# Rounding double-precision weights with the sign in the exponent: a clamp and a sloped rectifier in place of magnitude, minimum and sign steps, under newly ordered lists

## The chip, the core and the metric

The kernel runs on one core of a Trainium2 chip. A core has a matrix engine (TensorE, PE in the profile), a vector engine (VectorE, DVE), a scalar engine with function tables (ScalarE, ACT), GpSimd (POOL) and SyncE (SP), which here only issues transfers. Each engine works through its own list of instructions in order and waits on semaphores. The metric is device microseconds (us) of one execution. Three runs of the kernel before took 552.08, 551.65 and 548.6 us: the median is 551.65.

## The reference

Two layers stand behind one another. The first is a gated linear recurrence with complex gates, per batch (4) and head (8), over 768 steps with states of 48x48; the second is a maxout layer on its output.

```python
for t in range(S):                       # S = 768, D = 48
    ar, ai = (a_re_n[:, :, t, :, None], a_im_n[:, :, t, :, None])
    new_re = ar * S_re - ai * S_im
    new_im = ar * S_im + ai * S_re
    S_re, S_im = (new_re + kv, new_im)   # kv: outer product of k[t], v[t]
    y[:, :, t] = np.einsum('bhd,bhde->bhe', q[:, :, t], S_re)
# second layer: x is y as (3072, 384)
h = np.maximum(np.maximum(x @ w1, x @ w2), x @ w3)   # w1..w3: (384, 768)
return (h @ w_out).astype(np.float32)                # w_out: (768, 384)
```

The gates are first limited to a magnitude of 0.999. The four weight matrices come in double precision (64 bits each); q, k, v and the gates are single precision.

## The kernel before, in words

**Groups and chunks.** Time is cut into 12 groups (g = 0 to 11) of 64 steps. A group has two chunks, x and y, of two batch rows each. For each group the gates' logarithms and phases are worked out ("gates" and "angles": Square, Ln, Exp, Relu, Arctan and Sin on ScalarE, products on VectorE), summed along time by matmuls (`sums`, `cs`, `F`), and turned into factors. Then k and q are scaled, transposed (`tp`), scored against one another (`A`, `B`), masked into `atm`, and multiplied with v and the carried state (`y`, `dk`, with states in `g`).

**The second layer.** It is computed as x·w1·w_out plus max(0, x(w2-w1), x(w3-w1))·w_out. So w1 is kept negated, added to w2 and w3 (step g below), and the product w1·w_out (`wp`) is formed once (`T`, `t`, `M`, `m` words: transposes `wt`, products `wm`). `U..` words are the up matmuls into `up`, `u..` words take the maximum; from group 1 on the output matmuls run as seven products of half size (`P1` to `P7`, sums `S1` to `S4` in the tile called strassen, additions `r..`, `ox`, `oy`, `oz`).

**Weights.** There are 12 blocks (0 to 11) of 128 partitions x 768 weights: 0, 3, 6 of w1, 1, 4, 7 of w2, 2, 5, 8 of w3, 9 to 11 of w_out. `weight_load` (word `WL`) brings a raw block of 768 KB into a room that several blocks share (`ROOMS`): H and S, the upper parts of w2, w3 and w_out. Each weight lies there as two 32-bit words, low and high. `weight_step` (line 419 on) then rounds it to single precision, one word of the list for each step:

- a: ScalarE writes the magnitude of the high word, read as a float and scaled by 2^-112, into `ex` (a part of the tile xhx that two blocks take turns in, `EX`).
- b: VectorE takes the minimum with LAST.
- c: VectorE shifts left by three bits, which makes the 64-bit exponent a 32-bit one; for w1 it also sets the sign bit.
- e: VectorE puts the top three bits of the low word underneath.
- f: VectorE brings in the sign of the high word and writes the weight to its place.
- g: for w2 and w3 only, the block of w1 is added, on VectorE or by an adding transfer of POOL.

**Order.** No scheduler decides the order. `SCHEDULE` (line 21 on) is a list of words such as `Wb3:0` (step b of block 3) or `Ax:2` (scores of chunk x of group 2); `program` runs it from left to right, and each engine gets its instructions in that order (the class `Bound` ties each to the one before). `SLOTS` gives each PSUM tile one of four slots. `OTHER` is a set of words that run on their second engine: magnitudes and copies on VectorE instead of ScalarE, loads of q, k, v on POOL's queue instead of SP's, additions on VectorE instead of an adding transfer of POOL. `activation` loads a new table on ScalarE when the next function is in the other one of two sets (Exp and Ln in one, Sin and Arctan in the other); Abs, Relu, Square and Copy run in either.

Nearly all instructions carry line 198, that of the recording helper, so groups are told apart by their tiles.

Of the kernel before, what the change touches and what calls it, by code (L numbers as in the profile page):

```python
# [26 lines left out]
xor:1 Enx:0 Eqx:0 lnL:1 Wc9:0 Ekx:0 tx:0 relu:1 mkx:0 csy:0 expe:1 We9:0 nfx:0 expw:1 sumsy:0 Lix:2 ty:0 Wf9:0 abs:1
T2:0 nfy:0 mqx:0 half:1 afx:0 Wa10:0 Wa11:0 Lvy:0 t2:0 Wb10:0 Wb11:0 Wc10:0 Wc11:0 We10:0 sax:0 We11:0 pw:1 sbx:0
uqx:0 tpqx:0 lnw:1 t0:0 Wf11:0 WL1:0 T1:0 WL2:0 Wf10:0 expL:1 Qcx:0 Lky:0 ukx:0 tpkx:0 mulw:1 Wa1:0 t1:0 Cdx:0 Lvx:0
Eqy:0 Kcx:0 Wa2:0 lne:1 Q2x:0 Fy:0 f2y:0 Wb1:0 f1y:0 WL4:0 kEnx:0 Q1x:0 M0:0 f3y:0 Liy:2 f0y:0 Eny:0 mulai:1 Wb2:0  # L30
afy:0 Ax:0 Wc1:0 stt:1 We1:0 mqy:0 Wc2:0 Wf1:0 We2:0 Eky:0 say:0 QBx:0 sqi:2 KBx:0 Lnop:1 sby:0 Wa4:0 Wf2:0 g0x:0
dkx:0 Lrx:2 Lry:2 sqr:2 add:2 atan:1 lnL:2 Wb4:0 Cdy:0 turn:1 WL5:0 Wg1:0 Wc4:0 M1:0 h1x:0 expe:2 cs:1 relu:2 g1x:0
Liy:3 expw:2 t:1 Wa5:0 abs:2 lne:2 We4:0 g2x:0 mky:0 Wf4:0 uky:0 M2:0 g3x:0 Bx:0 Wb5:0 nfx:1 Wc5:0 m1:0 Z3:0 b1x:0
tpky:0 Zh:0 uqy:0 nfy:1 b0x:0 tpqy:0 We5:0 Wg4:0 Lix:3 F:1 Kcy:0 yx:0 Lqy:1 Qcy:0 Wf5:0 xor:2 m0:0 Q2y:0 xx:0 addw:2
Q1y:0 KBy:0 WL7:0 f1:1 f0:1 QBy:0 Wg2:0 sumsx:1 Enx:1 WL8:0 half:2 Cdx:1 Ekx:1 Cdy:1 U11x:0 u11x:0 Lqx:1 lnw:2 Ay:0
Wa7:0 g0y:0 Eqx:1 expL:2 af:1 U01x:0 Wb7:0 f2:1 u01x:0 U02x:0 g1y:0 By:0 mulai:2 Wg5:0 g2y:0 Wc7:0 Wa8:0 g3y:0 We7:0
b0y:0 Lky:1 b1y:0 kEny:0 Wf7:0 sumsy:1 f3:1 yy:0 mulw:2 xy:0 sb:1 dky:0 u02x:0 stt:2 U02y:0 Lkx:1 h1y:0 Z4:0 mqx:1
atan:2 U11y:0 Lnop:2 Wb8:0 mkx:1 turn:2 sa:1 ukx:1 u11y:0 U01y:0 U12y:0 u01y:0 Eky:1 uqx:1 u02y:0 Eqy:1 cs:2 u12y:0
tpqx:1 Wc8:0 We8:0 mky:1 Eny:1 Lky:2 tpkx:1 Qcx:1 Wf8:0 t:2 Wg7:0 U21y:0 Wg8:0 U21x:0 nfy:2 nfx:2 Q1x:1 Lqx:2 mqy:1
Q2x:1 kEnx:1 uqy:1 u21y:0 U22y:0 u22y:0 u21x:0 af:2 Kcx:1 sumsx:2 F:2 Ax:1 g0x:1 g1x:1 g2x:1 Ekx:2 Enx:2 Eqx:2 Z2:0  # L40
Lvx:1 f1:2 f3:2 KBx:1 h0x:1 uky:1 tpqy:1 f2:2 Qcy:1 Q1y:1 g3x:1 Oy:0 Lvy:2 tpky:1 Q2y:1 mqx:2 Lvy:1 f0:2 Lkx:2 sa:2
sqi:3 oy:0 Lry:3 J3:0 QBx:1 dkx:1 Bx:1 sb:2 h1x:1 U12x:0 QBy:1 uqx:2 QGx:1 U22x:0 Kcy:1 KBy:1 Lrx:3 Lqy:2 u22x:0
u12x:0 Ay:1 b1x:1 g0y:1 g1y:1 g2y:1 g3y:1 b0x:1 mkx:2 sqr:3 tpqx:2 Qcx:2 By:1 yx:1 add:3 lnL:3 QBx:2 expe:3 b0y:1
sumsy:2 xx:1 Eqy:2 Eky:2 expw:3 relu:3 Q1x:2 b1y:1 QGy:1 abs:3 Ox:0 Q2x:2 Lix:4 ukx:2 ox:0 mky:2 mqy:2 Dy:0 uky:2 yy:1
addw:3 tpky:2 lne:3 kEny:1 tpkx:2 Liy:4 Lnop:3 xy:1 xor:3 half:3 Cdy:2 Kcy:2 U11:1 Cdx:2 J1:0 U01:1 Lqx:3 Lrx:4 uqy:2
lnw:3 Kcx:2 KBx:2 J2:0 expL:3 u11:1 Dx:0 Eny:2 mulw:3 mulai:3 stt:3 kEny:2 h0y:1 tpqy:2 atan:3 Lry:4 sqi:4 turn:3
Qcy:2 dky:1 h1y:1 kEnx:2 sumsx:3 u01:1 J4:0 cs:3 Eqx:3 mqx:3 Ax:2 h0y:2 Ekx:3 t:3 sqr:4 add:4 g0x:2 g1x:2 g2x:2 U12:1
Enx:3 Lrx:5 nfx:3 U02:1 lnL:4 expe:4 Q1y:2 nfy:3 expw:4 u12:1 S3:1 af:3 dky:2 g3x:2 relu:4 abs:4 addw:4 Q2y:2 F:3
u02:1 Bx:2 Ay:2 Lvx:2 sb:3 S1:1 f2:3 Lkx:3 h1y:2 f1:3 QGx:2 Lqy:3 P5:1 S2:1 P7:1 f0:3 QBy:2 g0y:2 KBy:2 g1y:2 f3:3
S4:1 lnw:4 g2y:2 P1:1 expL:4 h0x:2 P6:1 r1:1 b0x:2 b1x:2 g3y:2 r6:1 dkx:2 r5:1 r7:1 lne:4 Lry:5 sa:3 Lky:3 r57:1 h1x:2  # L50
sumsy:3 By:2 xor:4 mkx:3 b1y:2 b0y:2 Eny:3 half:4 Cdy:3 Liy:5 yx:2 xx:2 mulw:4 Eky:3 Eqy:3 Py:1 QGy:2 Px:1 P4:1 P3:1
# [5 lines left out]
Qcx:4 dky:3 kEnx:3 dkx:3 S1:2 h1y:3 sumsy:4 S2:2 P5:2 h1x:3 Eqy:4 QBy:3 Dx:1 abs:5 Liy:6 addw:5 b0x:3 b1x:3 lne:5
Lnop:5 half:5 Eky:4 mky:4 Eny:4 mqy:4 Cdx:4 S4:2 Cdy:4 P1:2 P6:2 Py:2 P4:2 r1:2 yx:3 r6:2 r5:2 By:3 lnw:5 expL:5 b0y:3
mulw:5 uqy:4 h0x:4 b1y:3 mulai:5 QGy:3 Px:2 stt:5 atan:5 Lix:6 P3:2 Lry:6 xx:3 sqr:6 Liy:7 P7:2 r7:2 Lkx:5 uky:4 P2:2
tpqy:4 Lky:5 Qcy:4 r57:2 tpky:4 yy:3 sqi:6 ox:2 Lqx:5 kEnx:4 kEny:4 Lvx:4 dkx:4 oy:2 add:6 xy:3 Kcy:4 sumsy:5 turn:5  # L60
sumsx:5 h1x:4 QGx:4 Dy:2 Dx:2 Ekx:5 cs:5 Q1y:4 lnL:6 Lix:7 Eqx:5 U11:3 mkx:5 expw:6 Lvx:5 relu:6 KBx:4 Q2x:4 Enx:5
expe:6 lne:6 h0y:4 Q2y:4 mqx:5 Eky:5 U01:3 Lnop:6 abs:6 Q1x:4 u11:3 t:5 nfy:5 nfx:5 Eny:5 QBx:4 u01:3 Eqy:5 mky:5
xor:6 Ax:4 af:5 g0x:4 addw:6 sb:5 dky:4 h1y:4 sa:5 F:5 half:6 f3:5 uqx:5 g1x:4 g2x:4 lnw:6 expL:6 U12:3 u12:3 f2:5
Lrx:7 f0:5 f1:5 U02:3 tpqx:5 g3x:4 mulai:6 uky:5 tpky:5 Qcx:5 mulw:6 u02:3 Lqy:5 S1:3 Ay:4 Bx:4 S2:3 P1:3 QBy:4 sqi:7
S3:3 mqy:5 b1x:4 P5:3 Kcy:5 b0x:4 KBy:4 g0y:4 P6:3 stt:6 g1y:4 uqy:5 By:4 atan:6 yx:4 ukx:5 P7:3 g2y:4 g3y:4 Lkx:6
Lry:7 sqr:7 QGy:4 b0y:4 b1y:4 Cdy:5 Cdx:5 Q1x:5 tpkx:5 xx:4 Kcx:5 turn:6 tpqy:5 add:7 S4:3 Qcy:5 Lvx:6 r1:3 yy:4 xy:4
sumsx:6 Eqx:6 cs:6 t:6 lnL:7 r6:3 Px:3 kEnx:5 r5:3 Q2x:5 Py:3 P4:3 Enx:6 h0x:5 Ekx:6 xor:7 nfy:6 kEny:5 P2:3 U01:4
r7:3 nfx:6 expw:7 dkx:5 expe:7 lne:7 relu:7 abs:7 r57:3 addw:7 QGx:5 af:6 Lry:8 Lvy:5 h1x:5 mqx:6 sb:6 Lqy:6 u01:4
sumsy:6 QBx:5 sa:6 F:6 Liy:8 U11:4 f3:6 Eqy:6 mkx:6 Q2y:5 Eky:6 KBx:5 mqy:6 P3:3 Lky:6 Q1y:5 f1:6 uqy:6 Lrx:8 h0y:5
f0:6 oy:3 Eny:6 ox:3 Bx:5 u11:4 KBy:5 lnw:7 Ax:5 g0x:5 Ay:5 g1x:5 half:7 g2x:5 expL:7 f2:6 g3x:5 mulai:7 U02:4 g0y:5  # L70
g1y:5 g2y:5 b0x:5 g3y:5 QBy:5 b1x:5 mky:6 yx:5 ukx:6 By:5 Lvy:6 Dx:3 Cdy:6 u02:4 Cdx:6 QGy:5 mulw:7 b1y:5 uqx:6 U12:4
P1:4 S3:4 b0y:5 P7:4 stt:7 atan:7 Lqx:7 xx:5 u12:4 S1:4 tpqx:6 tpkx:6 S2:4 Kcx:6 yy:5 turn:7 Lnop:7 dky:5 Qcx:6 uky:6
Lkx:7 r1:4 sqr:8 sumsx:7 xy:5 h1y:5 cs:7 t:7 kEnx:6 Lix:8 sqi:8 P6:4 Px:4 Py:4 P5:4 P2:4 P4:4 QBx:6 Dy:3 h0x:6 add:8
lnL:8 relu:8 Q1x:6 expw:8 nfx:7 Q2x:6 Eqx:7 expe:8 S4:4 nfy:7 P3:4 tpqy:6 r6:4 KBx:6 Lqx:8 abs:8 Liy:9 r5:4 r7:4 Ekx:7
r57:4 tpky:6 ox:4 oy:4 Enx:7 af:7 dkx:6 Qcy:6 kEny:6 F:7 Dx:4 sa:7 xor:8 h1x:6 half:8 sb:7 h0y:6 Lkx:8 Dy:4 f0:7 f2:7
Q2y:6 f1:7 QGx:6 U11:5 u11:5 Cdx:7 mkx:7 U12:5 Kcy:6 u12:5 Q1y:6 Lry:9 Cdy:7 U01:5 Lrx:9 Lix:9 mqx:7 addw:8 f3:7 ukx:7
# [994 lines left out]
```

## Time and profile before

| what | before |
|---|---|
| runs, us | 552.08, 551.65, 548.6 |
| profiled execution, span in us (no other time of it is given) | 550.3 |
| TensorE (PE) busy, us | 515.6 |
| VectorE (DVE) busy, us | 484.8 |
| ScalarE (ACT) busy, us | 363.8 |
| GpSimd (POOL) busy, us | 115.6 |
| table loads on ScalarE | 50, 64.2 us |
| transfers | 47.93 MB |

A row of groups reads: line, engine, operation, output tile <- input tiles, partitions x elements, count, then busy time, mean of one in ns, and idle time before it with what ended it. A row of a table by stretches reads: the stretch, its length, then busy time and instruction count of each engine, the clock that TensorE was granted (1.00 is full), the share of the transfer engines and GB/s. A row of waits reads: who waited, for whom, us in total, times, longest. A row in order of time reads: start, duration, engine, operation and tiles, count.

### The profile page before, as it was taken

Reading aid. Unit: us, or ns where it says so; the run is one execution under the profiler, and the core shown is the slowest. Engines: PE = TensorE matmul, PEld = TensorE weight load, DVE = VectorE, ACT = ScalarE, POOL = GpSimd, SP = SyncE. Lnnn points to the kernel's source line nnn. Section 1 sums busy time; section 2 is a strip of 40 time slices with the busy share of each in tenths; the row PEclk is TensorE's granted clock in tenths of the full one; section 3 lists DMA queues with packets and bytes.
Section 4 is the critical chain, followed back from the end, with each engine's and each line's share of the span. In section 5 each row is a group of like instructions: output and inputs, shape, how many; then the busy total and the mean of one; then the engine's idle time right before and its main releaser. Section 6 shows DMA issues by size and latency. Waiting matters only on the chain.

```text
span 550.3 us, 22368 instructions
## 1 busy us (share of the span) xinstructions
PE 515.6 (94%) x9998; PEld 441.4 (80%) x9998; DVE 484.8 (88%) x735; ACT 363.8 (66%) x568; POOL 115.6 (21%) x167
## 2 busy tenths in 40 slices
PE   2478989999999999999999999999999899999996
PEld 1245578778988888988898988988988788988886
DVE  7999989999999999999999999988999687886325
ACT  6999898688989778696492638677678465221000
POOL 7524180030251222214004001303101250000000
PEclk9769899999999999999999999999999899999999
DMA  8978975553443455244516025356150350010011
GB/s 233 243 206 170 244 129 89 101 92 69 80 89 74 96 111 104 49 91 83 104 42 121 3 52 107 64 105 112 22 104 11 66 117 2 4 30 4 2 29 29
DMA packets 117023, 47.93 MB, mean 87 GB/s; under 512 B 103936, under 2 KB 109536, under 8 KB 116928
## 3 DMA queue, kind: packets, MB, share of 16 engines
q1 hardware_dynamic: 104272, 31.87, 27.4%
q0 software_dynamic: 10304, 14.05, 14.1%
q8 instruction: 78, 1.28, 0.9%
q10 hardware_dynamic: 2352, 0.59, 0.5%
q14 instruction: 17, 0.14, 0.1%
HBM read 33.03 MB, written 4.72 MB: 69 GB/s over the span
## 4 chain that ended last, share of the span: by engine, by line
PE 71%; DVE 10%; issue 2%; ACT 1%; DVEq 0%; ACTq 0%
PE up L198 28%; PE op L198 22%; PE y L198 6%; PE tp L198 4%; PE A L198 3%; PE dk L198 3%; PE sums L198 2%; DVE atm L198 1%; PE B L198 1%; DVE Q L198 1%; PE F L198 1%; DVE QG L198 1%; PE cs L198 1%; DVE uk L198 1%; DVE xhx L198 1%
## 5 line engine op out<-in xcount | busy, mean ns | idle before, releaser
L198 PE MATMUL up<-xhx,w 128*128 128x256 f32 x792 | 177.5, 382 | 0.0
L198 PEld LDWEIGHTS up<-xhx,w 128*128 128x128 f32 x792 | 148.6, 190 | 22.4 <-DVE g L198 2.2
L198 ACT ACT_TABLE_LOAD x50 | 64.2, 1283 | 4.4 <-issue 3.6
L198 POOL DMA_DIRECT2D ar<-nf x44 | 39.9, 1297 | 77.8 <-DVE ar L198 66.7
L198 ACT COPY atm<-B 32x128 f32<-32x128 f32 x96 | 24.5, 256 | 39.4 <-DVE atm L198 24.2
L198 PE MATMUL op<-wo,xhx 128*128 128x192 f32 (+1 forms) x220 | 49.2, 362 | 0.0
L198 DVE TENSOR_TENSOR Q<-Q,f 112x1024 f32<-112x1024 f32 (+1 forms) x48 | 45.3, 951 | 0.4 <-ACT Q L198 0.2
L198 PE MATMUL y<-atm,vb 128*32 128x64 f32 x1152 | 39.4, 221 | 2.9 <-issue 2.9
L198 PEld LDWEIGHTS op<-wo,xhx 128*128 128x128 f32 x220 | 36.7, 190 | 3.3 <-issue 0.6
L198 PEld LDWEIGHTS y<-atm,vb 128*32 128x32 f32 x1152 | 33.1, 110 | 7.3 <-issue 6.2
L198 PE MATMUL y<-QG,g 112*32 112x64 f32 x1408 | 37.3, 220 | 0.5 <-issue 0.5
L198 DVE TENSOR_TENSOR ot<-ot,op 128x192 f32<-128x192 f32 (+1 forms) x67 | 27.1, 413 | 11.0 <-PE op L198 6.2
L198 DVE TENSOR_TENSOR xhx<-xhx,up 128x768 f32<-128x768 f32 x22 | 20.9, 951 | 17.9 <-PE up L198 17.9
L198 PEld LDWEIGHTS y<-QG,g 112*32 112x32 f32 x1408 | 34.6, 110 | 0.7 <-issue 0.7
L198 PE MATMUL op<-wo,strassen 128*128 128x192 f32 x176 | 34.2, 339 | 0.1
L198 POOL DMA_DIRECT2D w<-L x8 | 9.0, 1124 | 117.4 <-ACT L L198 104.8
L198 PE MATMUL op<-w,strassen 128*128 128x192 f32 x176 | 32.8, 329 | 0.0
L198 DVE COPY_PREDICATED atm<-masko,A 128x256 f32<-128x256 uint8 x72 | 31.2, 435 | 1.2
L198 PEld LDWEIGHTS op<-wo,strassen 128*128 128x128 f32 x176 | 30.0, 196 | 2.3 <-issue 0.7
L198 PE MATMUL A<-Q,K 112*32 112x80 f32 x1536 | 30.6, 234 | 0.5 <-issue 0.5
L198 PEld LDWEIGHTS op<-w,strassen 128*128 128x128 f32 x176 | 28.9, 190 | 1.9 <-ACT ot L198 0.8
L198 PEld LDWEIGHTS A<-Q,K 112*32 112x32 f32 x1536 | 27.4, 110 | 3.6 <-issue 1.4
(156 smaller groups left out, 1114.5 us busy)
## 6 DMA issues: line engine op xcount, KB each, us to landing
...
w<-in_moe_w_dram SPq DMA_DIRECT2D x3, 768.0 KB, 7.0
```

The source lines that it names most:

```text
L198: ins = f(*a, **kw)
```

## The change

Steps a, b, c and f change; f is gone, and the order is now b, a, c, e, g.

- b reads the high word itself, as a float with its sign, and holds it between -LAST and LAST (two operations in one instruction). LAST is now unscaled.
- a is ScalarE's rectifier with a slope (Prelu): positive values are scaled by 2^-112, negative ones also by -2^32, so that their magnitude stands 32 binades higher. For w1 the scale is negative, which exchanges the two.
- c shifts left by three bits; the 32 in the exponent moves into the sign bit. The form for w1 that set the sign is not needed.
- e puts the low bits underneath and writes the weight straight to its place.

`SCHEDULE`, `SLOTS` and `OTHER` are all new, about 100 lines. In the built program the matmuls are the same in number; VectorE has 13 instructions fewer and ScalarE 7 fewer, 6 of them table loads (50 to 44). Two more of step g (blocks 4 and 8) go to POOL as adding transfers. Early magnitudes (`abs1:0`, `afy:0`, `abs:1`, `abs:2`) and one maximum (`u11x:0`) go to VectorE from ScalarE. In the last group `oz` and its transfer `Dz` stand ahead of `ox`, `Dx`, `oy`, `Dy` instead of behind them.

```diff
-    LAST = float(np.array(0x0FEFFFFF, dtype=np.int32).view(np.float32))
+    LAST = float(np.array(0x47EFFFFF, dtype=np.int32).view(np.float32))
...
-        if step == "a":
-            activation(out=ex.bitcast(FP), in_=high.bitcast(FP), func=AF.Abs, scale=2.0 ** -112)
-        elif step == "b":
-            dve.tensor_single_scalar(out=ex.bitcast(FP), in_=ex.bitcast(FP), scalar=LAST, op=OP.min)
+        if step == "b":
+            dve.tensor_scalar(out=ex.bitcast(FP), in0=high.bitcast(FP), scalar1=LAST, scalar2=-LAST, op0=OP.min, op1=OP.max)
+        elif step == "a":
+            activation(out=ex.bitcast(FP), in_=ex.bitcast(FP), func=AF.Prelu, alpha=-2.0 ** 32,
+                       scale=-2.0 ** -112 if i in (0, 3, 6) else 2.0 ** -112)
         elif step == "c":
-            if i in (0, 3, 6):
-                dve.tensor_scalar(out=ex, in0=ex, scalar1=3, scalar2=-0x80000000, op0=OP.logical_shift_left,
-                                  op1=OP.bitwise_or)
-            else:
-                dve.tensor_single_scalar(out=ex, in_=ex, scalar=3, op=OP.logical_shift_left)
+            dve.tensor_single_scalar(out=ex, in_=ex, scalar=3, op=OP.logical_shift_left)
         elif step == "e":
-            dve.scalar_tensor_tensor(out=ex, in0=low, scalar=29, in1=ex, op0=OP.logical_shift_right, op1=OP.bitwise_or)
-        elif step == "f":
-            dve.scalar_tensor_tensor(out=dst.bitcast(I32), in0=high, scalar=-0x80000000, in1=ex,
-                                     op0=OP.bitwise_and, op1=OP.bitwise_xor)
+            dve.scalar_tensor_tensor(out=dst.bitcast(I32), in0=low, scalar=29, in1=ex, op0=OP.logical_shift_right,
+                                     op1=OP.bitwise_or)
```

The beginning of the list of words, before and after (the whole of it is exchanged in this manner):

```diff
-Lix:0 sqi0:0 Zf:0 Zg:0 Lrx:0 xor0:0 sqr0:0 Liy:0 Lry:0 sqi1:0 add0:0 lnL0:0 expe0:0 expw0:0 xor1:0 lne0:0 relu0:0
-Lnop0:0 WL0:0 sqr1:0 Wa0:0 add1:0 CL:0 lnL1:0 expe1:0 Lkx:0 abs0:0 Lix:1 Wb0:0 Wc0:0 We0:0 WL3:0 half0:0 expw1:0 Fx:0
+Lix:0 Lrx:0 Zg:0 Liy:0 sqi0:0 sqr0:0 Lry:0 sqi1:0 add0:0 lnL0:0 sqr1:0 Zf:0 expe0:0 add1:0 xor0:0 expw0:0 lne0:0
+relu0:0 WL0:0 Wb0:0 Lnop0:0 WL3:0 WL6:0 lnL1:0 abs0:0 Wa0:0 xor1:0 Wc0:0 expe1:0 pw0:0 sumsx:0 expw1:0 Lry:1 lne1:0
...
-r57:11 Dx:11 oy:11 Dy:11 oz:11 Dz:11
+P5:11 P7:11 S4:11 P6:11 r6:11 P3:11 P4:11 r5:11 r7:11 r57:11 oz:11 Dz:11 ox:11 Dx:11 oy:11 Dy:11
```

More of the change, by code (lines that the diff above doesn't have):

```diff
@@ L27 @@
[L27 to L51, printed above, removed]
@@ L57 @@
[L57 to L76, printed above, removed]
@@ new lines @@
+Eqx:0 Liy:1 half1:0 expL1:0 stt0:0 mulai1:0 Wb6:0 mulw1:0 Wc3:0 Fx:0 f1x:0 f0x:0 stt1:0 atan0:0 turn0:0 We3:0 sqr:1
+WL9:0 Wa6:0 sumsy:0 atan1:0 sqi:1 Lkx:0 csx:0 turn1:0 csy:0 tx:0 add:1 nfx:0 WL10:0 CL:0 Wb9:0 mkx:0 f2x:0 ty:0 Wc6:0
+We6:0 lnL:1 nfy:0 Wa9:0 Wc9:0 Wb10:0 afx:0 WL11:0 T1:0 relu:1 We9:0 WL1:0 afy:0 T2:0 expe:1 expw:1 Wb11:0 WL2:0 abs:1
+t2:0 xor:1 Wa10:0 Lqx:0 Wc10:0 Wa11:0 f3x:0 Wc11:0 Lqy:0 sax:0 sbx:0 We10:0 pw:1 half:1 We11:0 ukx:0 mqx:0 lnw:1 t1:0
+T0:0 Wb1:0 uqx:0 expL:1 Lvx:0 tpkx:0 Lky:0 Wb2:0 mulw:1 mulai:1 t0:0 WL4:0 Lvy:0 tpqx:0 Lix:2 Liy:2 Lry:2 Kcx:0 Wa1:0
@@ new lines @@
+sumsx:2 F:2 h1x:1 nfx:2 Ax:1 nfy:2 Wg8:0 U22y:0 Enx:2 Eqx:2 f3:2 Ekx:2 f0:2 af:2 QGx:1 sb:2 g0x:1 sa:2 QBx:1 KBx:1
+kEny:1 f2:2 u22y:0 Lkx:2 f1:2 Q2y:1 mqx:2 Oy:0 g1x:1 U22x:0 Lrx:3 mkx:2 ukx:2 uqx:2 Q1y:1 g2x:1 tpqx:2 g3x:1 u22x:0
+oy:0 tpkx:2 Qcx:2 Bx:1 b1x:1 J3:0 b0x:1 Lry:3 KBy:1 Ay:1 Liy:4 g0y:1 Kcx:2 QBy:1 sqi:3 yx:1 Q1x:2 g1y:1 sqr:3 add:3
+lnL:3 expe:3 expw:3 QGy:1 relu:3 g2y:1 By:1 Ox:0 Q2x:2 J1:0 Lqy:3 g3y:1 b1y:1 abs:3 h0y:1 xx:1 b0y:1 yy:1 xor:3 J2:0
+QGx:2 half:3 addw:3 sumsy:2 dky:1 xy:1 lne:3 ox:0 Lix:4 lnw:3 Dy:0 Lvy:3 Eqy:2 h1y:1 kEnx:2 Lrx:4 Eky:2 U11:1 U01:1
@@ new lines @@
+kEny:3 U02:2 U12:2 sumsy:4 b1x:3 b0x:3 h0x:3 sa:4 Q2y:3 uqx:4 lne:5 u02:2 u12:2 abs:5 Eky:4 KBy:3 Eny:4 Lvx:3 Eqy:4
+S1:2 ukx:4 dkx:3 tpqx:4 Qcx:4 S2:2 yx:3 Ay:3 addw:5 lnw:5 By:3 h1x:3 g0y:3 P1:2 S3:2 Lnop:5 Dy:1 r1:2 P5:2 g1y:3 g2y:3
+g3y:3 Px:2 QGy:3 xx:3 P6:2 Lky:4 half:5 P2:2 b1y:3 S4:2 P7:2 sqr:6 mky:4 Liy:6 Cdy:4 expL:5 mulai:5 Dx:1 Py:2 P3:2
+mulw:5 r6:2 Q1x:4 stt:5 Lqy:4 b0y:3 Liy:7 uky:4 atan:5 P4:2 Lix:7 Cdx:4 r5:2 sqi:6 yy:3 tpky:4 mqy:4 xy:3 uqy:4 r7:2
+r57:2 tpqy:4 Qcy:4 ox:2 oy:2 turn:5 h0y:3 Q2x:4 tpkx:4 F:5 add:6 kEnx:4 U11:3 f0:5 Kcy:4 dkx:4 h0x:4 Kcx:4 Lrx:7 Dx:2
@@ new lines @@
+Lky:5 Q2y:4 f1:5 f2:5 f3:5 sumsy:5 QGx:4 Lry:7 KBx:4 u11:3 cs:5 Lvx:5 Eky:5 Eqy:5 sumsx:5 Eny:5 t:5 h1x:4 lnL:6 nfy:5
+nfx:5 Q1y:4 xor:6 mky:5 dky:3 Ax:4 kEny:4 g0x:4 expw:6 expe:6 h1y:3 relu:6 U12:3 abs:6 mqy:5 g1x:4 Eqx:5 af:5 sa:5
+QBx:4 u12:3 Lqx:5 mqx:5 sb:5 uky:5 lne:6 U01:3 g2x:4 addw:6 half:6 Cdy:5 g3x:4 h0y:4 lnw:6 uqx:5 Ekx:5 uqy:5 U02:3
+expL:6 Enx:5 mulai:6 tpqx:5 u01:3 Dy:2 Bx:4 b1x:4 b0x:4 u02:3 Lnop:6 Ay:4 QBy:4 Qcx:5 yx:4 S3:3 KBy:4 g0y:4 S1:3 By:4
+g1y:4 mulw:6 sqr:7 S2:3 g2y:4 P1:3 mkx:5 g3y:4 P7:3 P5:3 P6:3 Px:3 QGy:4 Cdx:5 S4:3 b0y:4 r1:3 sqi:7 Py:3 add:7 r6:3
@@ new lines @@
+P2:5 addw:9 uky:7 oy:5 P3:5 lnw:9 expL:9 tpky:7 ox:5 tpqy:7 nfx:8 dky:6 sumsx:8 mulai:9 h1y:6 Qcy:7 mulw:9 KBx:7 af:8
+Lqx:8 half:9 Dy:5 Lqy:8 Dx:5 Lky:9 Lrx:10 dkx:7 U11:6 Lkx:8 Lry:10 h0x:7 Lvx:8 Ekx:8 Eqx:8 Q2y:7 u11:6 sqi:10 Enx:8
+QGx:7 lne:9 U12:6 kEny:7 mkx:8 u12:6 stt:9 sa:8 sb:8 Q1y:7 h1x:7 Kcy:7 U01:6 ukx:8 Q2x:7 Cdx:8 U02:6 atan:9 sumsy:8
+Lnop:9 Lky:8 sqr:10 u01:6 F:8 Cdy:8 Eky:8 u02:6 mqx:8 Ax:7 S1:6 Ay:7 Eny:8 f2:8 f3:8 Eqy:8 S3:6 add:10 g0y:7 f1:8 f0:8
+Bx:7 g0x:7 g1x:7 S2:6 P1:6 g2x:7 mqy:8 g3x:7 r1:6 g1y:7 P5:6 g2y:7 mky:8 P6:6 b1x:7 Py:6 uqx:8 g3y:7 b0x:7 P4:6 turn:9
```

120 lines of the change are left out of this document (69 added, 51 removed).

## The prediction

> **What bounds the kernel now.** I read the page first, then the table by stretches, then PE's waits, then single instructions in order of time.
>
> ```profile
> span 550.3 us, 22368 instructions
> PE 515.6 (94%) x9998; PEld 441.4 (80%) x9998; DVE 484.8 (88%) x735; ACT 363.8 (66%) x568; POOL 115.6 (21%) x167
> PE   2478989999999999999999999999999899999996
> DVE  7999989999999999999999999988999687886325
> ACT  6999898688989778696492638677678465221000
> PEclk9769899999999999999999999999999899999999
> ```
>
> PE is busy 94% of the span, but its row rises only over the first five slices; there DVE and ACT are the full ones. The stretches are cut at two matmul groups that recur below.
>
> ```profile
> 76.39 1.14 PE L198 MATMUL dk<-vb,uk 64*64 64x48 f32 x64
> 93.56 2.20 PE L198 MATMUL op<-wo,xT 128*128 128x384 f32 x6
> 0.00:76.39 76.39, 50.17 (x738) 32.60 (x739) 70.44 (x123) 68.61 (x112) 36.87 (x71) 0.87 0.88 208
> 76.39:93.56 17.17, 16.40 (x355) 14.93 (x348) 16.79 (x26) 14.24 (x23) 4.50 (x6) 1.00 0.80 129
> 93.56:220.00 126.44, 125.52 (x2680) 106.58 (x2678) 123.83 (x181) 106.27 (x156) 27.71 (x36) 1.00 0.47 89
> 220.00:546.20 326.20, 323.51 (x6236) 287.28 (x6234) 273.11 (x406) 174.69 (x279) 46.49 (x57) 0.99 0.29 56
> ```
>
> Columns after the length: PE, PE's weight loads, DVE, ACT, POOL, clock, transfers. Until 76.39 us PE is idle for 26.2 us, DVE for 6.0 and ACT for 7.8, most of that at the start. From 76.39 to 546.20, where the last matmul ends, PE is idle for only 4.4 us of 469.8. So the kernel is a preparation that VectorE and ScalarE bound together, and then a PE that hardly stops. DVE stays 98% busy to 220 us, so it could bound PE again up to there; later it has room. What PE waits for after 76.39 (the first four rows are those to 220 us, the last one those behind):
>
> ```profile
> PE y L198 <- issue: 0.5, 1, 0.5
> PE tp L198 <- ACT E L198: 0.4, 1, 0.4
> PE up L198 <- ACT hT L198: 0.3, 1, 0.3
> PE dk L198 <- DVE xhx L198: 0.2, 1, 0.2
> ...
> PE y L198 <- issue: 2.6, 1, 2.6
> ```
>
> Only some 1.4 us hang on preparation; the 2.6 us waited for nothing that the trace shows.
>
> **The change part by part.** Prices first: VectorE, in order of time and by groups, then ScalarE by groups.
>
> ```profile
> 37.21 0.95 DVE L198 SCALAR_TENSOR_TENSOR wo<-w,xhx 128x768 int32<-128x768 int32 x1
> 38.08 0.94 DVE L198 SCALAR_TENSOR_TENSOR wo<-strassen,xhx 128x768 int32<-128x768 int32 x1
> ...
> L198 DVE TENSOR_SCALAR xhx<-xhx 128x768 int32<-128x768 int32 x12 | 6.8, 574 | 0.0
> L198 DVE TENSOR_SCALAR xhx<-xhx 128x768 f32<-128x768 f32 x12 | 6.7, 558 | 0.4 <-ACT xhx L198 0.4
> L198 DVE SCALAR_TENSOR_TENSOR xhx<-w,xhx 128x768 int32<-128x768 int32 x4 | 3.8, 949 | 0.0
> L198 DVE SCALAR_TENSOR_TENSOR w<-w,xhx 128x768 int32<-128x768 int32 x3 | 2.8, 945 | 0.0
> L198 DVE TENSOR_TENSOR hT<-hT,up 128x256 f32<-128x256 f32 x6 | 2.4, 416 | 0.1
> L198 DVE TENSOR_SCALAR L<-ar 128x768 int32<-128x768 int32 x3 | 1.7, 556 | 1.0 <-ACT Ln L198 1.0
> L198 DVE TENSOR_SCALAR e<-ar 128x384 int32<-128x384 int32 x1 | 0.4, 410 | 0.0
> L198 DVE TENSOR_SCALAR af<-nf 128x384 int32<-128x384 int32 x1 | 0.4, 353 | 0.0
> ```
>
> ```profile
> L198 ACT ACT_TABLE_LOAD x50 | 64.2, 1283 | 4.4 <-issue 3.6
> L198 ACT COPY atm<-B 32x128 f32<-32x128 f32 x96 | 24.5, 256 | 39.4 <-DVE atm L198 24.2 <-PE B L198 14.1
> L198 ACT COPY K<-tp 112x1024 f32<-112x1024 f32 x21 | 21.1, 1014 | 7.4 <-PE tp L198 7.2
> L198 ACT COPY Q<-tp 112x1024 f32<-112x1024 f32 x18 | 18.3, 1017 | 3.4 <-PE tp L198 3.2
> L198 ACT ACTIVATE e<-e,biases 128x768 f32<-128x768 f32 x11 | 10.3, 937 | 0.1
> L198 ACT ACTIVATE L<-ar 128x768 f32<-128x768 f32 x8 | 6.7, 843 | 0.1
> L198 ACT ACTIVATE xhx<-w 128x768 f32<-128x768 f32 x4 | 3.6, 905 | 0.0
> ```
>
> Two full VectorE instructions of 0.95 us start 0.87 apart, so an instruction gives back its duration less 0.08; one of 0.56 gives 0.48. On ScalarE I take 0.04 off. I then compare the two built orders at the same matmul group: which instructions of VectorE and ScalarE its semaphores make it wait for, in each order.
>
> *Step f* goes: 12 x 0.87 = 10.4 us of VectorE. *Step c* loses its form for w1; both forms lie in the one row of 574 ns, so nothing changes. *Step e* writes elsewhere at 945 to 949 ns, as before. *Step b* now reads every second word. The trace has no one-source instruction with such a source: below stands the contiguous b at 558 ns, above the two-source row xhx<-w,xhx, which reads every second word, at 949. A gain below 558 I exclude, since the work is at least that of the old b. I take 558, the row of the same kind of instruction; the other end costs 12 x 0.39 = 4.7 us more. *Step a*: magnitude cost 905 ns with every second word read; contiguous functions of 768 lie at 843, with a bias from memory at 937. No row shows the sloped rectifier; I take 843 (12 x 0.06 = 0.7 us less ScalarE) and keep 937 as the upper end, which would cost 0.4 us against before. *The handoffs*: b to a to c is one engine crossing more than a to b to c. VectorE has steps of other blocks between, and no cover is needed while it is full; where it is not, a wait of ScalarE's 0.84 us per block would show.
>
> A row of the same kind decides b for me. The Trainium skill (VectorE: DVE Perf Modes, What auto-detection actually checks) speaks for the same end: two elements a cycle ask for one source and a destination in SBUF with even or equal outer dimensions, and the step between elements is no condition. No trace here shows that; by it the sum is the one with 558, and without it the one with 949.
>
> *First place, `dk` of chunk y of group 0 (76.39 us).* VectorE instructions ahead of it: 122 before (the stretch above counts 123), 113 after. The difference: ten f -8.75; one e and one c fewer -1.37; one addition of w1, now POOL's, -0.88; one product that now comes later -0.88; four magnitudes and one maximum taken over from ScalarE +1.91. Sum -9.9 us, or -5.6 with a slow b (11 of them). ScalarE: 112 before, 99 after. Twelve magnitudes of weights become eleven of a: -1.64; five other magnitudes (four now VectorE's, one later) -3.36; four copies into atm, two activations of 768 and one of 256 now later -2.80. Sum -7.8. PE has one group `y` less ahead of the place, 0.7 us, so that much more behind. PE's end would come 9.2 (4.9) us earlier by VectorE, 7.1 by ScalarE.
>
> *Second place, the first `op` (93.56 us).* VectorE 147 to 141: twelve f -10.5, two additions of w1 -1.76, taken over +1.91, three other instructions pulled ahead +2.63: -7.7, or -3.0 with a slow b. ScalarE 133 to 130: the same five magnitudes -3.36, weights -0.84, one maximum -0.34, a copy of K, one of Q and a factor pulled ahead +2.46: -2.1. PE has one `dk`, one `tp` and one small `up` more done before it, together 2.9 us. PE's end: 10.6 (5.9) us earlier by VectorE, 5.0 by ScalarE.
>
> The least of these counts, since each place bounds the end by itself: 5.0 us, by ScalarE; with a slow b 4.9, by VectorE. So the price of b hardly moves the forecast. What is late next is ScalarE, and the six table loads that go cannot help there: both orders have 7 loads ahead of the first place and 9 ahead of the second. Behind 220 us VectorE and ScalarE have room (273 and 175 of 326 us), so the rest of the new order costs nothing unless a wait of its own arises; if that cover fails, each instruction out of place costs PE up to its 0.95 us.
>
> *Waits behind the first place.* Of the 1.4 us, shorter lists should take half: 0.7.
>
> *Loads.* Fewer steps hold a raw block (b reads the high words first, e ends it), so a room comes free 0.87 us sooner. SP's queue waits for such rooms:
>
> ```profile
> SPq L198 <- DVE w L198: 56.9, 9, 20.5
> SPq L198 <- DVE wo L198: 11.0, 2, 7.0
> ```
>
> Behind these stand loads of gates, k and q on SP; they come sooner or not later. Blocks 3 and 6 now load ahead of the gates of group 1. POOL issues 14 transfers more and SP 12 fewer; POOL is busy for 115.6 of 550 us, so this costs nothing. b now waits for the landing of its block on VectorE, where a used to wait on ScalarE; see the rivals.
>
> *The end.* Behind the last matmul:
>
> ```profile
> 544.70 1.46 PE L198 MATMUL op<-w,xhx 128*128 128x192 f32 x8
> 546.21 0.62 DVE L198 TENSOR_TENSOR ot<-ot,op 128x192 f32<-128x192 f32 x2 [0.56 <-PE op L198]
> ```
>
> Two additions stand there; with `oz` ahead only `oy` is left: half of 0.62, so 0.3 us less. `ox` needs P3, which ends one such matmul group earlier, so its transfers leave ahead.
>
> **Sum:** 5.0 + 0.7 + 0.3 = 6.0 us. The profiled execution spans 550.3, so 544.3; the median of the runs is 551.65, 1.35 above it, so 545.6.
>
> **The rivals.**
>
> *More than that.* If the gap of 2.6 us, which no wait explains, does not come back, and ScalarE's idle time shrinks so that the first place (7.1) decides: 7.1 + 1.4 + 0.3 + 2.6 = 11.4, 540.2 us. For it: the runs spread from 548.6 to 552.08. Against: gaps of this kind may come anywhere in a new order.
>
> *The gain is eaten by the new order.* In the preparation the transfers are full, and the weights are most of what moves:
>
> ```profile
> 5.00:10.00 5.00, 0.00 (x0) 0.00 (x0) 2.51 (x7) 3.75 (x9) 4.29 (x15) 1.00 1.17 282
> strassen<-in_moe_w_out_dram SPq DMA_DIRECT2D x1, 768.0 KB, 14.1
> ```
>
> A block of 0.79 MB takes 2.8 us at 282 GB/s, and the one into strassen landed 14.1 us after its issue. If b of two blocks stands on VectorE until its block lands, 5.6 us go, all that queues behind it with them, and the kernel comes out at 551.3; with three, at 554. It is decided from 2 blocks on. Against: SP now issues blocks 9 and 10 with nothing in between that waits. The same holds if the new order makes PE wait elsewhere: 548 to 554.
>
> *Slower: the rectifier is dear.* If a slope needs a second pass, a takes 0.9 us more for each of 12 blocks, 10.8 us on ScalarE ahead of the second place: -2.1 + 10.8 - 2.9 = 5.8 us later, less 0.3 at the end: 557.2. It turns the gain into a loss from 0.42 us per block (5.0 / 12). For it: no row shows this function. Against: a magnitude and a logarithm of this size lie at 843 and 937 ns in the rows above. A table load for each would be as dear (1283 ns), but the built order has no load in front of any.
>
> **How the numbers follow.** Steps pay as summed, 543 to 548 us: 0.54. More than that: 0.10. Eaten: 0.23. Dear rectifier: 0.13. About 1% (5.5 us) is what a measurement of this kernel can tell from no change, so faster means below 546.1. Of the first case two thirds lie there (0.36), with the second 0.46 faster. Within 1%: 0.18 + 0.23 = 0.41. Slower: 0.13. The range from 540 to 553.5 leaves out the dear rectifier and the end of the eaten case.
>
> **What would show it.** Right: 12 instructions xhx<-w, strassen, wo, xhx on VectorE at about 0.56 us and none of the form w<-w,xhx beyond e; ScalarE's xhx<-xhx at about 0.84; `dk` of chunk y at about 70 us, and the first `op` at about 91; PE's idle time up to the first `dk` down from 26.2 to some 20 us. Wrong: VectorE waiting for a transfer before 70 us; xhx<-xhx on ScalarE near 1.8 us; waits of PE behind 100 us of more than 4 us in sum.

## The result, and the profile after

The changed kernel is slower: 598.34 us in the median of 4 runs (592.74 to 601.85), beside 550.58 us for the kernel before. The ratio is 1.083, with an interval of 1.077 to 1.090. One run of the changed kernel, 601.85 us, and one of `after_shift_36` below, 612.22 us, count as slow runs: the ratios leave them out, and without them the medians are 597.01 and 605.07 us. The forecast was 545.6 us. The profiled execution of the changed kernel is the one of 601.85 us, its span is 599.8.

The head of its page:

```profile
span 599.8 us, 22361 instructions
PE 524.9 (88%) x9998; PEld 448.1 (75%) x9998; DVE 472.8 (79%) x722; ACT 355.0 (59%) x561; POOL 124.8 (21%) x181
PE   3587899998799989789899789989899789799996
DVE  7997899887879779788798778788798777766423
ACT  6997888677678478487537644357375746231000
PEclk9688999998899989999999999999999999799998
```

VectorE and ScalarE have less to do than before, by 12.0 and 8.8 us. PE does the same 9,998 matmuls, but its row, once an almost unbroken line of nines, has sevens and eights to the end. The same stretches as in the prediction, cut at the same two matmul groups:

```profile
0.00:73.27 73.27, 47.66 (x690) 30.42 (x694) 62.13 (x117) 62.45 (x104) 29.56 (x63) 0.88 0.97 227
73.27:94.56 21.29, 19.87 (x496) 18.51 (x485) 20.04 (x30) 19.34 (x30) 9.72 (x11) 1.00 0.62 106
94.56:220.00 125.44, 114.27 (x2252) 95.21 (x2250) 105.59 (x153) 87.45 (x134) 29.11 (x37) 0.96 0.46 87
220.00:546.20 326.20, 296.08 (x6095) 261.96 (x6095) 265.38 (x393) 182.82 (x287) 56.36 (x70) 0.99 0.28 55
```

The first `dk` of chunk y stands at 73.27 us (76.39 before), but PE has done 2.5 us less by then, so 0.6 us is won; at the first `op` (94.56, before 93.56) nothing is left of it: PE has been idle for 27.0 us in both kernels. All of the loss lies behind. From the first `op` to the end, before and after:

```profile
93.56:550.30 456.74, 449.03 (x8915) 393.86 (x8912) 397.56 (x588) 280.96 (x434) 74.20 (x91) 1.00 0.34 65
```

```profile
94.56:599.80 505.24, 457.39 (x8822) 399.19 (x8820) 390.59 (x578) 273.22 (x429) 85.47 (x107) 0.98 0.30 59
```

That is 48.5 us more: 40.1 us of idle PE (47.9 instead of 7.7) and 8.4 us of busier PE with 93 matmuls fewer, at a granted clock of 0.98 instead of 1.00. It begins at once: up to 220 us PE is idle for 11.2 us of this stretch, where before had 0.9. What the idle PE waited for in this stretch of the changed kernel:

```profile
PE y L196 <- issue: 10.9, 8, 2.4
PE op L196 <- DVE ot L196: 7.0, 4, 3.3
PE op L196 <- ACT ot L196: 5.5, 6, 2.4
PE F L196 <- issue: 5.2, 6, 1.6
PE B L196 <- issue: 3.4, 3, 1.8
PE dk L196 <- issue: 3.0, 2, 1.7
PE tp L196 <- DVE ot L196: 2.6, 2, 1.4
```

"Issue" is time in which nothing that the profile shows held PE: 24.0 us in 22 stops with the smaller rows, where before had 3.1. Waits for another engine come to 17.9 us (0.6 before). VectorE and ScalarE have room all the time, so this isn't a lack of throughput. It is two separate things.

**Stops in which nothing is missing but the program.** One of them lies inside a single group of matmuls of one shape, in order of time:

```profile
156.04 0.23 PE L196 MATMUL y<-atm,vb 128*32 128x64 f32 x2
156.05 0.33 PE L196 MATMUL y<-QG,g 112*32 112x64 f32 x9
158.78 0.25 PE L196 MATMUL y<-atm,vb 128*32 128x64 f32 x2 [2.40 <-issue]
```

PE's instructions come by a transfer queue of their own, and the page's third part counts its packets:

```profile
q8 instruction: 78, 1.28, 0.9%
```

78 packets make 1.28 MB, 16 KB each. The trace has 20,137 rows of PE (weight loads, matmuls, semaphores), 256 to a packet. I number them in order of time and take each stop of over 0.3 us behind 60 us. Six of them, worked out from the trace, with the packet of instructions that was under way:

```
packet starts   PE stops   PE resumes   group   row of PE, modulo 256
 72.2            74.0       74.6        dk      193
103.7           105.1      106.1        y       194
156.6           156.4      158.8        y       194
211.6           212.4      213.9        F       193
329.5           330.2      332.0        B       194
549.2           550.7      551.8        y       193
```

Of the 38 stops 25, with 28.6 us together, begin at row 193 or 194 modulo 256; the other 13 are spread over 13 other rows, with 16 us together. PE goes on 2.2 to 2.8 us after the packet's start. So PE reaches the end of the program that it holds while the next block is still on its way. The small matmuls make that possible: a group like `y` or `A` mostly uses some 120 to 140 rows in a microsecond, one like `up` or `op` 9 to 13. In 19 of the 25 the packet starts 0.6 to 1.6 us after PE has passed the row 256 ahead of the block's need, so I take it that the block is asked for there. In five it is 2.0 to 3.2 us, with other transfers on half of the transfer engines or more meanwhile; in the last of the table it is 7.1 us with none, which stays unexplained. From that row to PE's going on it is 2.9 to 4.4 us in 21 of them. With `up` and `op` in those rows there is time in plenty, with small groups in a row there is not. That the stops are the program's is shown by the experiments; when exactly it is asked for is only read from the times. The Trainium skill (Runtime: NRT & Kernel Launch, Instruction fetch mechanics) has the blocks of 16 KiB, with which the packets agree; that crossing their border is "mostly hidden" held for the kernel before and doesn't hold here.

**The clock behind a long stop.** Stretches of 2 us around that stop:

```profile
156.00:158.00 2.00, 0.38 (x28) 0.22 (x16) 2.00 (x4) 0.75 (x2) 0.67 (x1) 1.00 0.60 112
158.00:160.00 2.00, 1.22 (x48) 1.10 (x48) 2.00 (x3) 0.00 (x0) 0.00 (x0) 0.94 0.67 123
160.00:162.00 2.00, 2.00 (x7) 1.18 (x4) 1.53 (x3) 1.79 (x3) 1.59 (x3) 0.50 0.27 50
162.00:164.00 2.00, 2.00 (x9) 1.51 (x8) 0.46 (x1) 1.98 (x4) 2.00 (x5) 0.71 0.32 52
```

Worked out from these shares, the clock is halved for 3.4 us: 2.4 us of stop cost some 1.7 us more. Between the first `op` and the last matmul the clock records of the trace have four such stretches, from 146, 160, 214 and 518 us on, 17.1 us together, so some 8.5 us of work at full clock; before has one of 3.4 us behind its long stop. The difference, 6.8 us, is most of the 8.4 us of busier PE. The stretches at 160 and 214 us follow program stops of 2.4 and 1.6 us, the other two the waits of 2.45 and 3.3 us that come next.

**Waits of a new kind.** The other part is waits of PE for a step that reads an accumulator (a tile of two banks in PSUM) between two matmul groups that write it:

```profile
141.74 0.81 PE L196 MATMUL op<-w,strassen 128*128 128x192 f32 x4
145.00 1.26 PE L196 MATMUL op<-w,strassen 128*128 128x192 f32 x6 [2.45 <-ACT ot L196]
```

Here `r1:1` (a copy of the accumulator by ScalarE) stands between `P6:1` and `P7:1` in the list, and P7 has to wait until the copy has read. The place alone doesn't make the wait: counted in the two lists, 15 steps stand so in the new one and 13 in the old one, where the trace shows no wait of PE for any of them. In the new list the next group often follows at once, as here, and I read it that the reading engine comes late there; no run shows this apart.

### The profile page after: what moved, and what is told of

The parts are those of the page before. It is cut to its first block, busy times and chain, and to the rows that moved or that the text cites. A ratio compares the mean times of both kernels' runs of the same rounds, so it can differ in the third digit from the quotient of the medians.

```text
span 599.8 us, 22361 instructions
## 1 busy us (share of the span) xinstructions
PE 524.9 (88%) x9998; PEld 448.1 (75%) x9998; DVE 472.8 (79%) x722; ACT 355.0 (59%) x561; POOL 124.8 (21%) x181
## 3 DMA queue, kind: packets, MB, share of 16 engines
q8 instruction: 78, 1.28, 0.9%
## 5 line engine op out<-in xcount | busy, mean ns | idle before, releaser
L196 POOL DMA_DIRECT2D ar<-nf x44 | 44.6, 1516 | 53.7 <-DVE ar L196 51.5
L196 PE MATMUL op<-wo,xhx 128*128 128x192 f32 (+1 forms) x220 | 52.0, 376 | 0.8 <-issue 0.8
L196 PE MATMUL y<-atm,vb 128*32 128x64 f32 x1152 | 40.9, 224 | 8.0 <-issue 6.9
L196 PEld LDWEIGHTS y<-atm,vb 128*32 128x32 f32 x1152 | 33.2, 111 | 15.3 <-issue 12.5
L196 PE MATMUL y<-QG,g 112*32 112x64 f32 x1408 | 39.3, 221 | 4.0 <-issue 4.0
L196 POOL DMA_DIRECT2D w<-L x8 | 7.5, 934 | 141.7 <-ACT L L196 84.6
L196 ACT ACTIVATE xhx<-up 128x768 f32<-128x768 f32 x17 | 13.7, 810 | 34.4 <-PE up L196 30.3
```

The costliest lines, as they stand in the source:

```text
L196: ins = f(*a, **kw)
```

## The experiments

Theories: **S** (supply), the new lists put runs of small matmuls across the ends of program blocks; **W** (waits), PE is held by the steps that read an accumulator between its groups; and against both, that the new steps themselves cost the time. Each run is compared with runs of the kernel before on the same chip, whose medians lay between 550.6 and 551.9. No run leaves work out.

### Steps or lists?

`steps_alone`: the new steps in the old lists, b at the old place of a, a at that of b, f left out.

```diff
-Lnop0:0 WL0:0 sqr1:0 Wa0:0 add1:0 CL:0 lnL1:0 expe1:0 Lkx:0 abs0:0 Lix:1 Wb0:0 Wc0:0 We0:0 ...
+Lnop0:0 WL0:0 sqr1:0 Wb0:0 add1:0 CL:0 lnL1:0 expe1:0 Lkx:0 abs0:0 Lix:1 Wa0:0 Wc0:0 We0:0 ...
```

> The new weight steps in the lists of before: words Wa and Wb change names, the words Wf go, SLOTS and OTHER are those of before. Theory S (supply): in the slow kernel TensorE runs dry at instruction 449 + 256 k of its trace, 26 times behind 60 us, for 0.7 to 2.6 us each, because the next 256 instructions of its program arrive too late where many small matmuls stand; the new order caused that. Theory W (waits): the new order makes TensorE wait for additions of VectorE and ScalarE. Both put the loss on the lists, so both expect 540 to 549 us here (the 6 us of the prediction, or part of them). Theory D (dear steps): the new steps b and a, or their handoffs, cost the time: 575 us or more.

Measured: 556.78 us, ratio 1.011 (1.008 to 1.015). `lists_alone`: the old steps in the new lists, f behind e.

> The old weight steps (a, b, c, e, f) in the lists of after; f stands directly behind e. S and W expect the whole loss here: 592 to 608 us (after's 598, plus what twelve steps f of 0.87 us add in the preparation). D expects about 551 us.

Measured: 607.69 us, ratio 1.101 (1.097 to 1.105). The lists make the whole loss (the order, the slots and the second engines together; they were not tried apart), and the steps do two opposite things: in the old lists they cost 6 us, in the new ones they save some 10 (607.7 to 597.0). So the loss is not the steps' price, but S and W both expected a gain in the old lists, which did not come. Behind the first `op`, `steps_alone` is as fast as before:

```profile
97.79:554.50 456.71, 448.81 (x8916) 393.54 (x8912) 397.37 (x588) 280.43 (x434) 74.21 (x91) 1.00 0.34 65
```

456.7 us both times; `lists_alone` takes 505.3 there, the changed kernel 505.2. What the steps cost in the old lists stands ahead of that, in VectorE's, ScalarE's and PE's waits:

```profile
DVE xhx L196 <- ACT xhx L196: 5.4, 6, 1.8
ACT xhx L196 <- DVE xhx L196: 3.0, 2, 2.1
PE sums L196 <- ACT E L196: 5.4, 1, 5.4
```

b, a and c now pass from VectorE to ScalarE and back, and both engines wait for each other: c comes before a is done.

`b_early`: in the old lists, b directly ahead of a, both at a's old place, so that a is no later in the list than it was.

```diff
-... sqr1:0 Wb0:0 add1:0 CL:0 lnL1:0 expe1:0 Lkx:0 abs0:0 Lix:1 Wa0:0 Wc0:0 We0:0 ...
+... sqr1:0 Wb0:0 Wa0:0 add1:0 CL:0 lnL1:0 expe1:0 Lkx:0 abs0:0 Lix:1 Wc0:0 We0:0 ...
```

> The new weight steps in the old lists once more, with step b of each block directly ahead of a (where a stood before) and not directly ahead of c. In the first run of the new steps in the old lists VectorE stood 5.4 us at c for a, and the preparation came out 4 us late. Theory H (handoff): those waits ate the 10.4 us that the steps f gave back; with b early a is done when c comes, and the kernel is 543 to 549 us. Theory N (no gain to be had): what bounds the preparation is not VectorE's work, and the kernel is 551 to 557 us whatever the place of b.

Measured: 558.0 us, ratio 1.013 (1.010 to 1.015), no gain. The wait changed sides:

```profile
ACT xhx L196 <- DVE xhx L196: 7.3, 6, 2.1
DVE xhx L196 <- ACT xhx L196: 0.7, 3, 0.3
```

`b_early_five_abs` gives ScalarE's five early steps to VectorE as the change does (`abs1:0 afy:0 abs:1 abs:2 u11x:0` in `OTHER`).

> The new steps in the old lists with b early (558.0 us), and five magnitudes and maxima of the preparation taken from ScalarE to VectorE, as the new lists have them. Theory A (once VectorE's steps f are gone ScalarE bounds the preparation, with the wait for b on top): 550 to 555 us. If neither engine's work bounds it but the chain through both: 556 to 559 us.

Measured: 559.65 us, ratio 1.013 (1.009 to 1.018), and ScalarE waits 9.3 us for b in 7 places. The relief of ScalarE brought nothing, so I read it that the chain through both engines holds, not the load of one; a program stop of 3.8 us ahead of the first `op`, where `b_early` has 2.6, blurs the comparison. The new steps need an order of their own; the new lists give it to them (these waits are 0.1 us there), but lose elsewhere.

### Is it where the program's blocks end?

`shift_128` leaves the order of the kernel before untouched and puts 128 empty instructions at the start of PE's program, half a block; `shift_256` puts 252 of them and one matmul of three columns that nobody reads, a whole block, so that the ends fall where they fell.

```diff
+    pe.addr_align(256, offset=193)
     program(SCHEDULE, 0)
```

> The kernel before, with nothing changed but 128 empty instructions ahead of TensorE's first one, while it is idle anyway: every later instruction moves by half a block of 256. S: the kernel before runs dry only once (2.6 us at 427.8 us) because its small matmuls happen to stand well against the block ends; moved by half a block, TensorE runs dry some 15 to 30 times and the time is 566 to 585 us, with the stops 128 instructions off in the old count. W and D: the order of work is the same, so 548 to 552 us.

> The kernel before with 256 slots more ahead of TensorE's first instruction (252 empty ones and one tiny matmul): a whole block. S: the block ends fall where they fell before, so 548 to 553 us. If the empty instructions themselves cost the time, it is as slow as the run moved by 128 or slower. W and D: 548 to 552 us.

Measured: `shift_128` 571.53 us, ratio 1.036 (1.033 to 1.040); `shift_256` 560.53 us, ratio 1.018 (1.015 to 1.021). PE's waits for "issue" behind 93 us with half a block, then the row of `shift_256` behind its first `op`:

```profile
PE y L198 <- issue: 6.1, 4, 3.4
PE dk L198 <- issue: 2.9, 4, 1.3
PE F L198 <- issue: 2.6, 3, 1.6
PE A L198 <- issue: 2.6, 3, 1.2
```

```profile
101.60:556.40 454.80, 447.61 (x8915) 392.43 (x8912) 397.43 (x588) 281.14 (x434) 74.21 (x91) 1.00 0.34 66
```

Half a block brings 15 us of such stops into an untouched order (3.1 before); a whole block brings none, and the part behind the first `op` takes 454.8 us. What `shift_256` loses it loses at the start: PE runs empty instructions one after the other, one in about 74 ns, 18.5 us for 252 of them, which is longer than the 10.8 us for which PE waits there anyway. I had taken them as nearly free.

`after_shift_36` and `after_shift_200` do the same to the changed kernel, with slots that are jumped over and not run.

```diff
+    pe.addr_align(256, offset=101, max_nops=0)
     program(SCHEDULE, 0)
```

> The changed kernel with 36 empty slots ahead of TensorE's first instruction, jumped over and not executed: every later instruction stands 36 places further in its block of 256. Theory S: the groups of small matmuls stand worse to the block ends by some 8 us of stops (counted on the trace of the changed kernel: for each block, how long the 300 instructions ahead of its end take against the 4.0 to 4.4 us from request to arrival); with the half-speed clock 605 to 612 us. If the stops only show a late engine: 595 to 600 us, as the changed kernel.

> The same with 200 empty slots. Theory S: by the same count the stops are 2 to 4 us fewer than in the changed kernel, and some 10 to 12 us fewer than in the run moved by 36: 592 to 596 us, 10 us or more under that run. If the stops only show a late engine: 595 to 600 us in both.

Measured: 605.07 us, ratio 1.095 (1.086 to 1.103), and 596.88 us, ratio 1.082 (1.077 to 1.087), just above what S expected of it. The medians of the same order of work are 8.2 us apart, though the two intervals overlap a little. The stops differ by only 3.6 us; behind the first `op` the clock is halved for 17.1 us in the first and for 6.8 in the second, worth another 5.1 us. Plainer is that the stops move with the slots (worked out as above, rows modulo 256):

```
kernel             stops at the block end   us in sum   rows
after              25                       28.6        193, 194
after, 36 slots    24                       31.3        158, 159
after, 200 slots   24                       27.7        250, 251
```

36 slots move the rows back by 35, 200 slots by 199. S is a cause by itself. None of the three places is a good one for the new lists; I take it that too many of their small groups stand in a row.

### Taking the stops away

`after_spread` puts 848 empty instructions inside large groups at 13 places, so that block ends fall into `up` and `op`.

```diff
+                if j == 1 and T["word"] in PADS:
+                    pe.addr_align(256, offset=PADS[T["word"]])
```

> The changed kernel, same order of all work; 13 times, inside a group of large matmuls where TensorE's instruction stream has time to spare, 16 to 72 empty instructions move the block ends out of the groups of small matmuls that follow (848 in all; about half of the stops cannot be reached so, since several groups of small matmuls stand in a row). S: the stops at 256 k + 449 fall from some 28 us to 12 to 16, the half-speed clock behind them with it, so 575 to 588 us. W: stops at these places are only where waits show; more instructions don't help, 596 us or more.

Measured: 625.62 us, ratio 1.135 (1.130 to 1.140). The stops at block ends fell to 13 with 14.6 us, as S wants; but the empty instructions, one in about 75 ns, showed as 14.0 us of waits of `op` (5) and 13.7 of `up` (6), and behind the first `op` the clock is halved for 47.8 us instead of 17.1. As a remedy it failed through my assumption that they cost nothing inside a large group.

`sums_behind` is for W: 15 steps that read an accumulator go behind its last group.

```diff
-P1:1 P6:1 r1:1 P7:1 g0y:2 P5:1 addw:4 ...
+P1:1 P6:1 P7:1 g0y:2 P5:1 r1:1 addw:4 ...
```

> The changed kernel with 15 words of its list moved: where an addition or copy that reads one of the two accumulators of a group (r1, r6, r5, oy) stood between matmul groups that write the same accumulator, it now stands behind the last of them; the order of TensorE's own work does not change, so neither do the block ends. Theory W: TensorE's waits for ot (op<-DVE ot 7.0, op<-ACT ot 5.5 us, and the half-speed clock behind the long ones) are the price of these places: they go, and 598 falls to 578 to 590 us. Theory S alone: the waits are hidden behind, or replaced by, the stops at 256 k + 449, which stay at some 28 us: 595 to 600 us.

Measured: 592.52 us, ratio 1.074 (1.071 to 1.078). The 12.5 us of `op` behind `ot` are gone, but

```profile
PE y L196 <- issue: 13.8, 10, 2.4
PE tp L196 <- DVE ot L196: 5.5, 5, 1.6
PE F L196 <- issue: 5.2, 5, 1.4
...
PE y L196 <- ACT atm L196: 2.4, 2, 1.4
PE dk L196 <- ACT Q L196: 2.0, 1, 2.0
```

half of it comes back as waits of `tp`, `y` and `dk` for what was put off, and "issue" rises from 24.0 to 29.6 us; I read this as a PE that is held up less and so runs dry more. The result lies between what W and S expected: 4 to 6 of the 12.5 us were to be had, and even that is barely clear of noise, since the interval of the changed kernel, 1.077 to 1.090, begins where this one ends.

`spread_by_branch` is `sums_behind` with 8 places at which 847 slots in all are jumped over.

```diff
+        if T["word"] in PADS:
+            pe.addr_align(256, offset=PADS[T["word"]], max_nops=0)
```

> The changed kernel with the 15 words moved as before (592.5 us), and at eight places of TensorE's stream (one at its start) 48 to 169 empty slots that a branch jumps over, so that they shift the block ends without being executed; 12 empty instructions at a time took 0.8 us, so the branch is to be the cheaper way. Theory S: of the 28.9 us of stops at 256 k + 449 some 11 stay, and the half-speed clock behind the others goes too: 568 to 578 us, unless a jump itself costs TensorE over 1 us, which its row would show. If the stops are only the place where late engines show, the same time comes out as other waits: 588 to 596 us.

Measured: 583.95 us, ratio 1.060 (1.056 to 1.065). "Issue" falls from 29.6 to 18.9 us and the time by 8.6 us against `sums_behind`, less than the 14 to 24 that I expected: the rows left are `y` 5.3, `dk` 4.9, `F` 2.9 and `A` 2.9 us.

`new_then_old` takes the first 360 words of the new lists and then the old order, with old slots.

> The new weight steps; the first 360 words of the new lists (the preparation, up to about 97 us), then the words that are left in the order of the old lists, with the old SLOTS and OTHER for them; seven empty instructions at TensorE's start put its later instructions where they stood before. Theory S (supply) and theory W (waits) both put the loss of the new lists behind the preparation: 545 to 553 us, with at most two stops of TensorE behind 100 us. If the new lists cost their time in the preparation too, or the new steps do not pay even in lists made for them: 556 us or more, as with the new steps in the old lists.

Measured: 559.72 us, ratio 1.016 (1.012 to 1.019). Behind the first `op` it takes 455.0 us, as the old order does: the steady loss is gone with the new order. The expectation failed in the preparation: the first `op` stands at 101.83 us, PE stops for its program for 2.79 and 1.21 us ahead of it, waits 3.85 us for ScalarE's `f` right at it and 2.04 us for ScalarE's `Q` behind it.

### The one stop of the kernel before

The prediction left a gap of 2.6 us at 427.8 us unexplained. It begins at row 449 + 256 x 62. POOL had just sent for two large transfers, and the packet of instructions starts only at 428.0:

```profile
424.38 0.94 POOL L198 DMA_DIRECT2D w<-L  x1 [30.91 <-ACT L L198]
424.98 1.77 POOL L198 DMA_DIRECT2D k<-in_k_dram  x2
426.36 1.34 POOL L198 DMA_DIRECT2D Ln<-e  x1
```

`one_transfer_less` takes the last of them away (`Lnop:11` to `OTHER`), `other_transfer` the first (`addw:11`, an addition on VectorE instead of the adding transfer; the load of k then moves up too).

```diff
-xy:11 u01:11 u11:11
+xy:11 u01:11 u11:11 addw:11
```

> The kernel before with one word (Lnop of group 11) added to OTHER: its addition of 384 KB is made by VectorE in place of a transfer of POOL. In the kernel before the only long stop of TensorE (2.6 us at 427.8 us) falls where POOL has 0.98 MB of transfers under way, and its fetch starts 4.8 us after the stream passed the place at which other fetches start 0.6 to 1.6 us later. Theory T (the fetch waits behind transfers): the stop shrinks below 1.5 us, the half-speed clock behind it goes, 546 to 549 us. If the fetch is late for another reason: the stop stays and VectorE's 0.95 us more make 550.5 to 552 us.

> The kernel before with addw of group 11 on VectorE (the word added to OTHER) and Lnop of group 11 on POOL as it was. In the run with Lnop on VectorE the late fetch stayed: the transfers w<-L (384 KB) and k (192 KB) had been issued 3.5 us before it started and filled all queues until then. POOL had waited 30.9 us for the data of this one addition, and what stands behind it on POOL came in one burst with it. Theory T (a fetch of TensorE's program waits behind transfers under way): without that addition POOL's transfers leave earlier, the fetch starts 0.6 to 1.6 us behind its place, the stop of 2.3 us at 426 us and the half-speed clock behind it go: 546 to 549 us. If the fetch is late for a reason of its own, the stop stays: 550 to 552 us.

Measured: `one_transfer_less` 550.93 us, ratio 1.001 (0.998 to 1.004), with a stop of 2.33 us: not the transfer that matters. `other_transfer` 548.35 us, ratio 0.996 (0.995 to 0.998). All its waits of PE behind 94 us:

```profile
PE y L198 <- issue: 0.7, 1, 0.7
PE tp L198 <- ACT E L198: 0.4, 1, 0.4
PE dk L198 <- DVE xhx L198: 0.2, 1, 0.2
```

With the two transfers out of the way the block comes in time but for 0.7 us, and the clock stays at 1.00. That the packet stood behind them is how I read the times; which of the two held it wasn't tried. This kernel is 0.4% faster than the one before.

## Why the prediction was wrong

- *Prices.* Right. Twelve b at 547 to 577 ns and a at 839, where 558 and 843 were taken:

```profile
L196 ACT ACTIVATE xhx<-xhx 128x768 f32<-128x768 f32 x12 | 9.9, 839 | 0.1
L196 DVE TENSOR_SCALAR xhx<-w 128x768 f32<-128x768 f32 x4 | 2.3, 577 | 0.1
L196 DVE TENSOR_SCALAR xhx<-strassen 128x768 f32<-128x768 f32 x3 | 1.7, 558 | 0.0
```

A block's b reads every second word and costs no more for it, as the Trainium skill's rule (VectorE: DVE Perf Modes, What auto-detection actually checks) had it. The rival of the dear rectifier fell: no second pass and no table load ahead of it.
- *Handoffs.* "VectorE has steps of other blocks between, and no cover is needed while it is full": right in the new lists (0.1 us of waits), wrong in the old ones (8 us of them in `steps_alone` and 8 in `b_early`).
- *First and second place, 5.0 us.* The instructions went as counted: up to the first place VectorE is busy for 8.3 us less and ScalarE for 6.2. But VectorE is idle for 11.1 us there instead of 6.0 and ScalarE for 10.8 instead of 7.8, and PE for 25.6 instead of 26.2. The count took the idle time of each engine as given; a new order makes its own (VectorE waits 3.4 us for a transfer into `ar`, 2.4 for ScalarE's `e` and 2.2 for PE's `A`). Worth 0.6 us at one place and nothing at the other.
- *The end, 0.3 us.* Three additions, not one, stand behind the last matmul, and from its end to the end of the span it is 5.4 us instead of 4.2.
- *The step that failed.* "Behind 220 us VectorE and ScalarE have room (273 and 175 of 326 us), so the rest of the new order costs nothing unless a wait of its own arises; if that cover fails, each instruction out of place costs PE up to its 0.95 us." The room was there, and the rest of the new order cost 48.5 us all the same. PE was held by two things that room says nothing of: its own program (24.0 us of "issue" instead of 3.1), and accumulators read halfway (12.5 of the 17.9 us of waits for other engines, which were 0.6). The price of one is also more than 0.95 us: stops took up to 2.4 us, waits up to 3.3, and the clock behind a long one adds to it.
- *The rival "eaten by the new order".* Its kind came true ("new order makes PE wait elsewhere"), but its 548 to 554 us are at most some 8 us above the forecast, and the kernel came out over 50 above it. Its place, blocks that land late under b, is not where the time went.
- *The gap of 2.6 us.* It was read as one "which no wait explains" and could "come anywhere in a new order". That sentence held the answer and was priced once, not per block: behind 76 us, before has two stops at block ends (0.5, which was counted with the 1.4 us that hang on preparation, and 2.6 us), the changed kernel 23. `other_transfer` shows that most of it could be removed.
- *What would show it wrong*, waits of PE behind 100 us of over 4 us, is what came. VectorE's wait for a transfer before 70 us came too (the 3.4 us, at 52 us), for the gates and not for weights.

How the 48 us split is not settled to the end. The waits of `op` behind `ot` are 12.5 us as the trace lists them and gave 4 to 6 when taken away; S has 28.6 us of stops, 3.5 of them ahead of the first `op`; the slower clock follows either kind; and two partial remedies took some 13 us together. Where the order has so many small groups in a row, no run showed the loss gone except with the old order in its place.
